# The opening of a two-layer kernel on one core: dummies read a constant, the first block of taps moves ahead of two late transposes, and the early filter turn is split

## The chip, the cores and the metric

The kernel runs on one core of one Trainium2 chip. The core has five engines with instruction streams of their own: PE (matrix multiply; its weight loads are shown as PEld), DVE (vector), ACT (scalar functions, copies), POOL and SP (which only issues transfers here). An engine works through its stream in the order in which the program was written; engines wait for each other through semaphores. The metric is the device time of one execution, in microseconds (us).

## The reference

Two layers, each a gated long convolution followed by a gated feed-forward block, over x of 2048 tokens by 576 channels, all in bf16:

```python
def _A_ref(q, k, v, shift_k, ssm_k, ssm_D):
    k_pad = jnp.pad(k, ((0, 0), (ks - 1, 0), (0, 0)))          # ks = 4 taps
    for t in range(ks):
        k_shift = k_shift + k_pad[:, t:t + S, :] * shift_k[:, ks - 1 - t][None, None, :]
    kv = k_shift * v
    y = irfft(rfft(kv, 2S) * rfft(ssm_k, 2S))[:S]               # along the tokens
    y = y + kv * ssm_D[None, None, :]
    return q * y

def _B_ref(x, w_gate, w_up, w_down):                            # 576 -> 4608 -> 576
    return (_gelu(x @ w_gate) * (x @ w_up)) @ w_down

x = A_q
x = x + _A_ref(_layernorm(x), A_k, A_v, A_shift_k, A_ssm_k, A_ssm_D)
x = x + _B_ref(_layernorm(x), B_w_gate, B_w_up, B_w_down)
x = x + _A_ref(_layernorm(x), A_k, A_v, A_shift_k, A_ssm_k, A_ssm_D)
x = x + _B_ref(_layernorm(x), B_w_gate, B_w_up, B_w_down)
```

The transforms are written out in the kernel as matmuls with tables of cosines and sines. The product with D is folded into the filter: D is added to its value at time 0.

## The kernel before

The 2048 tokens are cut into four blocks of 512. The convolution does block 0 first (`Conv.begin`, L836), as fast as it can, since the feed-forward block of the first 512 tokens needs its result. The other three blocks are then woven into the feed-forward matmuls, in an order that a planner (`Pace`, with estimated costs) writes down when the program is built. The change doesn't touch the planner, and nothing in `begin` that the change edits feeds it. The order within `begin` is written out by hand; each engine follows it.

A block of 512 tokens lies on 128 partitions with RT = 4 tokens each, so token i of a partition is one of 0 to 3. The 576 channels are four full blocks of 128 and one of 64 (nd = 4, `width`). What `begin` does on each engine, as far as the change and the steps below touch it:

- SP issues the loads: k of block 0 (L172), the filter's first 512 channels into `hn` (L875), its last 64 channels, also into `hn` (L876), v (L181), the tables `W`, and later the feed-forward weights.
- **Dummies** (`busy`, L893): matmuls of 128x256 with a result that nobody reads, eight at first and two a little later. They read `full`, a part of `wx[1]` that DVE sets to 1.0 (L867).
- **Tap columns**: matmuls of `sk9` with the identity (L901) give the taps per channel, `wcol`; others (L912) give the taps of the last channels along the partitions, `sx`. DVE makes diagonal matrices `dg` from `wcol` (L907): for channel blocks 0 and 1 all four taps, for block 2 the taps 2 and 3. ACT makes taps 0 and 1 of block 2 later (L970).
- **k turned**: twelve transposes (L930), copied by ACT into `kT` (L935): channel blocks 0 and 1 in one copy, block 2 in another.
- **Late filter turn**, `turn_h(…, 1)`: tokens 3 and 2 of the filter, eight transposes of full channel blocks and then two of the last 64 channels (L963). Then `turn_d` (L937): one small transpose of D (L940), ACT's copy into `dcol` (L942), POOL's addition to the filter at time 0 in `hn` (L944). Then ACT copies the late tokens to `hT0` (L966).
- **Blocks of taps** (`shift_taps`, L819): for each of the channel blocks 0, 1 and 2, seven matmuls of turned k with the diagonals, 2048 columns in all. Blocks 0 and 1 share the one bank pair of the pool `cps`; block 2 has one of the three of the pool `ps`.
- **Early filter turn**, `turn_h(…, 0)`: tokens 1 and 0, ten transposes, written between blocks 0 and 1 and copied by ACT (L966).
- The last 192 channels of the taps go through DVE instead (L948 to L954).
- DVE multiplies the blocks of taps by v (L990), in two instructions: blocks 0 and 1, then block 2.
- **Filter transform**: `even(0, 0)` and `even(0, 1)` (L228) use the tokens 0 and 2 of `hT0`, token 0 first. Then the **transform of kv**, `kfwd` (L219), then `odd` (L228 again), then DVE's differences (`apart`, L233) and products (L359 to L362).

`new()`, `small()`, `new_t()` and `small_t()` take the next bank pair of the pools `ps` (three) and `cps` (one); a bank pair is used again when its last reader is done.

Of the kernel before, what the change touches and what calls it, by code (L numbers as in the profile page):

```python
# [15 lines left out]
ACT = mybir.ActivationFunctionType  # L16
ALU = mybir.AluOpType
F32 = mybir.dt.float32
BF16 = mybir.dt.bfloat16
# [3 lines left out]
P = 128  # L23
# [63 lines left out]
class Conv:  # L87
# [748 lines left out]
    def begin(self, head, tables):  # L836

        tc, nc, D, KS = self.tc, self.nc, self.D, self.KS
        nd = D // P
        width = lambda db: min(P, D - db * P)  # L840
        with ExitStack() as es:
# [8 lines left out]
            nt = nd - 1  # L850
            DW = D - nt * P
            wcol = tmp.tile([P, nt, KS], F32, name="wcol")
            sx = tmp.tile([P, KS, DW], BF16, name="sx")
            warm = tmp.tile([P, 1], F32, name="warm")
# [5 lines left out]
            dg = head.scratch([P, nt, RT, P], "dg")  # L860
            kx = tmp.tile([P, RT + KS - 1, DW], BF16, name="kx")
            below = tmp.tile([P, P], BF16, name="below")
            wx = [tmp.tile([P, RT, DW], BF16, name=f"wx{i}") for i in range(2)]
            full = wx[1][:].rearrange("p i c -> p (i c)")[:, 0:256]

            twice = lambda src: src.unsqueeze(1).to_broadcast([NH, 2, src.shape[1]])
            nc.vector.memset(full, 1.0)  # L867
            nc.scalar.dma_start(out=sk9[:], in_=twice(self.sk.rearrange("(b p) j -> b (p j)", p=HP)))
            self.load_k(0, nc.sync)
            nc.scalar.dma_start(out=dv9[:], in_=twice(self.sD.rearrange("(b p) -> b p", p=HP)))  # L870
            nc.vector.memset(kT[:, :, :, 0:2], 0.0)
            nc.vector.memset(below[:, 0:1], 0.0)
            nc.vector.tensor_copy(out=below[:, 1:P], in_=self.ident[:, 0:P - 1])
            nc.scalar.activation(out=warm[:], in_=full[:, 0:1], func=ACT.Sqrt)
            nc.sync.dma_start(out=hn[:, 0:nd, :], in_=self.hk[0:nd * P, 0:BS].rearrange("(b p) t -> p b t", p=P))  # L875
            nc.sync.dma_start(out=hn[0:D - nd * P, nd, :], in_=self.hk[nd * P:D, 0:BS])  # L876
            self.load_v(0, nc.sync)
# [12 lines left out]
            new_t = lambda: self.psp.tile([P, 2, 1024], BF16, tag="pr", name="pt")  # L890
            small_t = lambda: self.cpsp.tile([P, 2, 1024], BF16, tag="cps", name="cpt")

            def busy(ps, n):  # L893
                for _ in range(n):
                    nc.tensor.matmul(ps[:, 0, 0:256], lhsT=full[:, 0:P], rhs=full, start=True, stop=True)
            idle = small()
            busy(idle, 8)
            ps = new()
            halves = ((0, HP), (HP, P))
            for j in range(KS):  # L900
# [9 lines left out]
            ps = new()  # L910
            for c in range(DW // HP):
                nc.tensor.matmul(ps[:, c // 2, c % 2 * HP * KS:(c % 2 + 1) * HP * KS],  # L912
                                 lhsT=self.ident[0:NH, 2 * nt + c:2 * nt + c + 1].to_broadcast([NH, P]),
                                 rhs=sk9[:, 0, :], start=True, stop=True)
            for e, (lo, hi) in enumerate(((0, P), (P, DW))):
                nc.scalar.copy(out=sx[:, :, lo:hi], in_=ps[:, e, 0:(hi - lo) * KS].rearrange("p (d j) -> p j d", j=KS))
            busy(idle, 2)
            k, v = self.kt_[0], self.vt_[0]
            rest = slice(nt * P, D)
# [4 lines left out]
            pts = []  # L924
            for n, dbs in enumerate(DBS):
                pt = new_t() if n else small_t()
# [6 lines left out]
            for dbs, pt in zip(DBS, pts):  # L933
                ne = len(dbs)
                nc.scalar.copy(out=kT[:, dbs[0]:dbs[-1] + 1, :, 2:P + 2],  # L935
                               in_=pt[:, 0:ne, 0:RT * P].rearrange("p e (u q) -> p e u q", u=RT))
            def turn_d(pt):  # L937

                at = RT * P
                nc.tensor.transpose(pt[:, 1, at:at + NH], dv9[:].rearrange("b h p -> b (h p)"), self.ident[0:NH, 0:NH])  # L940
                for h, (lo, hi) in enumerate(halves):
                    nc.scalar.copy(out=dcol[lo:hi, 0:(NH + 1 - h) // 2], in_=pt[lo:hi, 1, at + h:at + NH:2])  # L942
                for lo, hi, w in ((0, nd, P), (nd, nd + 1, D - nd * P)):
                    nc.gpsimd.tensor_tensor(out=hn[0:w, lo:hi, 0], in0=hn[0:w, lo:hi, 0], in1=dcol[0:w, lo:hi], op=ALU.add)  # L944
# [8 lines left out]
                tt(out=wx[0][:], in0=wx[0][:], in1=wx[1][:], op=ALU.add)  # L953
            tt(out=v[:, :, rest], in0=wx[0][:], in1=v[:, :, rest], op=ALU.mult)  # L954

            def turn_h(pt, g, first=None):

                hv = hn[:].rearrange("p b (q i) -> p b i q", i=RT)
                for dbs in (range(nd), (nd,)):
                    for i in (2 * g + 1, 2 * g):  # L960
                        for db in dbs:
                            w = width(db)
                            nc.tensor.transpose(pt[:, i % 2, db * P:db * P + w], hv[0:w, db, i, :], self.ident[0:w, 0:w])  # L963
                if first:
                    first()
                nc.scalar.copy(out=hT0[:, 2 * g:2 * g + 2, :], in_=pt[:, :, 0:D])  # L966

            turn_h(new_t(), 1, lambda: turn_d(pts[1]))
            for j in range(2):
                nc.scalar.activation(out=dg[:, nt - 1, j, :], in_=self.ident[:], func=ACT.Copy, scale=wcol[:, nt - 1, j:j + 1])  # L970
            out = []
            for n, dbs in enumerate(DBS):
                o = (new() if n else small())[:].rearrange("p e (i c) -> p e i c", i=RT)
                for e, db in enumerate(dbs):
                    self.shift_taps(k, kT, dg, P, db, o[:, e])
                    if db == 0:
                        turn_h(new_t(), 0)
                out.append(o)
            self.hT1 = head.scratch([P, RT, D], "hT1")[:]
            nc.sync.dma_start(out=self.hT1, in_=self.Td[1].rearrange("(p i) d -> p i d", i=RT))  # L980
            skT = tc.dram_tile([1, KS * D], BF16, name="skT")
# [904 lines left out]
```

## Time and profile before

| | |
|---|---|
| runs | 908.52, 909.13, 910.92 us (median 909.13) |
| span of the profiled execution | 908.5 us |
| busy share | PE 99%, PEld 58%, DVE 63%, ACT 36%, POOL 17% |
| the chain that ended last, by engine | PE 97%, DVE 2%, DMA 1% |
| first matmul of gate/up (end of the opening) | 35.22 us |

The span runs from the first to the last instruction of one profiled execution; which of the three times belongs to it is not noted. In the rows below, a timeline row is start, length, engine, line of the kernel, operation, output<-inputs, tile and count; in square brackets stands how long the engine was idle before and what ended this. Rows next to each other on the timeline can be several instructions merged. A row of the chain is start, length, and the engine and line that it ran through. A row of a group by shape is line, engine, operation, shapes, count, then busy us, mean ns of one, and idle us before. PE's matmuls are pipelined: a mean of 0.4 us and a step of 0.2 us from one to the next go together.

### The profile page before, as it was taken

To read this page: it belongs to the slowest core of one execution; us is meant where nothing else is said; L and a number is where in the kernel's file an instruction comes from. 1 tells how busy PE (TensorE), PEld (TensorE's weight loads), DVE (VectorE), ACT (ScalarE), POOL (GpSimd) and SP (SyncE) were. 2 spreads that over 40 slices of the span, in tenths; PEclk is the share of its full clock that TensorE was granted. 3 is DMA by queue.
4 is the path that set the end of the run, shared out by engine and by line. 5 is a ranking of instruction groups with operands and counts; after the bars stand their busy time and mean duration, and the time that the engine had idled before them with its cause. 6 is when DMAs were issued, how large, how long until landed. Compare 5 with 4: busy or idle time off the path is not lost.

```text
span 908.5 us, 19157 instructions
## 1 busy us (share of the span) xinstructions
PE 902.1 (99%) x8133; PEld 524.7 (58%) x8133; DVE 575.9 (63%) x984; ACT 328.8 (36%) x616; POOL 158.2 (17%) x336
## 2 busy tenths in 40 slices
PE   9999999999999999999999999999999999999998
PEld 6875646556465465564654655645646646556555
DVE  7989976688888884787898855443333335332332
ACT  6765455523223254443125133551121125321221
POOL 3333315120223031420104002310000003100000
PEclk9999999999999999999999999999999999999999
DMA  9999997666629319785915601961520721966620
GB/s 260 301 298 295 221 226 139 193 190 147 198 92 266 95 27 172 210 142 131 273 55 133 169 3 42 187 137 41 123 73 15 143 80 27 190 162 172 142 55 27
DMA packets 132075, 132.90 MB, mean 146 GB/s; under 512 B 46139, under 2 KB 123670, under 8 KB 131990
## 3 DMA queue, kind: packets, MB, share of 16 engines
q1 hardware_dynamic: 121728, 94.65, 46.2%
q0 software_dynamic: 10208, 37.02, 13.0%
q8 instruction: 63, 1.03, 0.5%
q14 instruction: 22, 0.18, 0.1%
q10 hardware_dynamic: 54, 0.01, 0.0%
HBM read 108.36 MB, written 12.39 MB: 133 GB/s over the span
## 4 chain that ended last, share of the span: by engine, by line
PE 97%; DVE 2%; DMA 1%; SPq 0%; issue 0%; ACT 0%; DVEq 0%
PE gu L1758 59%; PE dn L1792 31%; PE gu L1677 3%; PE cps L282 1%; PE ps L415 1%; DMA hn<-in_A_ssm_k_dram 1%; PE cps L415 1%; PE ps L282 0%; DVE yb L362 0%; PE cps L823 0%; DVE prod L359 0%; DVE h L233 0%; DVE prod L361 0%; PE xps L1477 0%; DVE v L990 0%; PE pt L963 0%
## 5 line engine op out<-in xcount | busy, mean ns | idle before, releaser
L1758 PE MATMUL gu<-xnT,wgu 64*128 64x512 bf16 x4968 | 540.7, 376 | 0.0
L1758 PEld LDWEIGHTS <-wgu 64*128 64x128 bf16 x4968 | 239.7, 94 | 294.4 <-issue 5.9
L1767 ACT ACTIVATE ga<-gu 128x512 f32<-128x512 f32 x258 | 153.9, 596 | 451.1 <-PE gu L1758 442.7
L1768 DVE TENSOR_TENSOR hT<-ga,gu 128x512 bf16<-128x512 f32 x258 | 177.0, 686 | 200.0 <-ACT ga L1767 198.4
L1792 PE MATMUL dn<-wd,hT 128*128 128x288 bf16 x2304 | 292.1, 286 | 0.0
L1792 PEld LDWEIGHTS <-hT 128*128 128x128 bf16 x2304 | 223.5, 98 | 65.6 <-issue 9.5
L1831 DVE TENSOR_TENSOR x_c<-x_c,dn 128x576 f32<-128x576 f32 x62 | 46.6, 752 | 55.3 <-PE dn L1792 54.9
L1230 POOL TENSOR_SCALAR nm<-s 128x1 f32<-128x1 f32 x56 | 20.4, 365 | 270.5 <-DVE x_c L1823 210.8
L1238 ACT ACTIVATE junk<-x_c,nm 128x576 bf16<-128x576 f32 x48 | 36.9, 768 | 28.0 <-POOL nm L1230 25.9
L560 POOL DMA_DIRECT2D hr<-Hd x32 | 17.4, 545 | 117.7 <-DVE prod L361 117.1
L1246 POOL TENSOR_TENSOR rstd<-ve,neghalf_t 128x1 f32<-128x1 f32 x58 | 36.8, 635 | 4.8
L1302 ACT ACTIVATE xn<-x_c,nb,rstd 128x576 bf16<-128x576 f32 (+1 forms) x48 | 28.6, 644 | 5.9 <-POOL nb L1250 5.7
L1245 POOL TENSOR_SCALAR ve<-ss 128x1 f32<-128x1 f32 x58 | 21.8, 375 | 45.9 <-ACT junk L1238 45.8
L1814 DVE TENSOR_TENSOR ob<-x_c,dn 128x576 bf16<-128x576 f32 x15 | 11.3, 754 | 29.0 <-PE dn L1792 29.0
L285 ACT COPY eo<-cps 128x576 f32<-128x576 f32 x29 | 18.6, 643 | 27.3 <-PE cps L282 24.1
L1656 ACT ACTIVATE ga<-gu 128x512 bf16<-128x512 f32 x26 | 15.5, 598 | 30.5 <-PE gu L1758 25.9
L1677 PE MATMUL gu<-xnT,wgu 64*128 64x256 bf16 x432 | 24.8, 269 | 0.3 <-ACT xnT L1484 0.3
L1677 PEld LDWEIGHTS <-wgu 64*128 64x128 bf16 x432 | 21.4, 94 | 3.2 <-issue 1.2
L362 DVE TENSOR_TENSOR prod<-prod 128x576 bf16<-128x576 bf16 x48 | 22.0, 458 | 1.7
L430 POOL DMA_DIRECT2D out_dram<-ob x12 | 6.7, 562 | 91.6 <-DVE ob L1814 91.6
L245 DVE SCALAR_TENSOR_TENSOR eo<-eo 128x576 f32<-128x576 f32 x22 | 16.3, 753 | 5.8 <-ACT eo L285 5.8
L1280 DVE SCALAR_TENSOR_TENSOR x_c<-g_t,rstd,x_c 128x576 f32<-128x576 f32 x16 | 13.0, 814 | 8.6 <-POOL rstd L1246 8.6
(182 smaller groups left out, 591.3 us busy)
## 6 DMA issues: line engine op xcount, KB each, us to landing
wgu<-in_B_w_gate_dram SPq DMA_DIRECT2D x45, 576.0 KB, 5.6
wd<-in_B_w_down_dram SPq DMA_DIRECT2D x30, 864.0 KB, 7.1
wgu<-in_B_w_up_dram SPq DMA_DIRECT2D x45, 512.0 KB, 7.6
hr<-Hd POOLq DMA_DIRECT2D x32, 288.0 KB, 5.0
kr<-Kd POOLq DMA_DIRECT2D x24, 288.0 KB, 5.3
Kd<-kc POOLq DMA_DIRECT2D x12, 288.0 KB, 6.2
k<-in_A_k_dram POOLq DMA_DIRECT2D x3, 1008.0 KB, 12.0
wgu<-in_B_w_up_dram SPq DMA_DIRECT2D x45, 64.0 KB, 7.7
```

The lines of the kernel that those rows point to most:

```text
L362: nc.vector.tensor_tensor(out=dst, in0=pr[:, 0, :], in1=pr[:, 1, :], op=ALU.subtract if part == 0 else ALU.add)
L1230: nc.gpsimd.tensor_scalar(out=v["nm"][:], in0=v["s"][:], scalar1=-1.0 / D, scalar2=None, op0=ALU.mult)
L1238: nc.scalar.activation(out=junk[:], in_=get_x(), func=ACT.Square, bias=v["nm"][:, 0:1], accum_out=v["ss"][:])
L1245: nc.gpsimd.tensor_scalar(out=ve[:], in0=v["ss"][:], scalar1=1.0 / D, scalar2=EPS, op0=ALU.mult, op1=ALU.add)
L1246: nc.gpsimd.tensor_tensor(out=v["rstd"][:], in0=ve[:], in1=neghalf_t[:, 0:1], op=ALU.pow)
L1302: nc.scalar.activation(out=xn[:, lo:hi], in_=x_c[c][:, j, 0:hi - lo], func=ACT.Identity, scale=v["rstd"][:, 0:1], bias=v["nb"][:, 0:1])
L1677: nc.tensor.matmul(pair[:, s, e * 256:(e + 1) * 256], lhsT=w[r0:r0 + HK, k, gi * P:(gi + 1) * P], rhs=xnT[r0:r0 + HK, blk_of[k], tok], sta ...
L1758: nc.tensor.matmul(pair[:, s, :], lhsT=w[r0:r0 + HK, k, gi * P:(gi + 1) * P], rhs=xnT[r0:r0 + HK, b, :], start=(k == 0), stop=(k == NKC - 1))
L1767: nc.scalar.activation(out=ga[:], in_=pair[:, 0, :], func=ACT.Gelu_apprx_tanh)
L1768: nc.vector.tensor_tensor(out=hT[:, fi, :], in0=ga[:], in1=pair[:, 1, :], op=ALU.mult)
L1792: nc.tensor.matmul(part[h][:, h, 0:HW], lhsT=hT[:, fi, at * P:(at + 1) * P], rhs=wd[2 * wb + fi // WT][:, fi % WT, h * HW:(h + 1) * HW], s ...
L1831: nc.vector.tensor_tensor(out=xh, in0=xh, in1=acc[:, :, 0:HW], op=ALU.add)
```

## The change

The dummies and the table-loading activation read a constant of ones, one element repeated, that the program sets up before it starts; the DVE memset goes, and ten dummies are issued at first, not eight. `turn_h` is cut into the transposes and the copy (`keep_h`). Of the late turn only the eight full transposes stay ahead of the blocks of taps. The two of the last 64 channels, the turn of D, the late copy and ACT's two diagonals of block 2 come after block 0. Of the early turn, token 1 (five transposes) comes after block 1 and token 0 (five) after block 2; one copy follows both.

```diff
-            full = wx[1][:].rearrange("p i c -> p (i c)")[:, 0:256]
+            ones = lambda n: nc.const_aps.tensor(1.0, [P, n], BF16)
...
-            nc.vector.memset(full, 1.0)
...
-            nc.scalar.activation(out=warm[:], in_=full[:, 0:1], func=ACT.Sqrt)
+            nc.scalar.activation(out=warm[:], in_=ones(1), func=ACT.Sqrt)
...
-                    nc.tensor.matmul(ps[:, 0, 0:256], lhsT=full[:, 0:P], rhs=full, start=True, stop=True)
+                    nc.tensor.matmul(ps[:, 0, 0:256], lhsT=ones(P), rhs=ones(256), start=True, stop=True)
             idle = small()
-            busy(idle, 8)
+            busy(idle, 10)
...
-            def turn_h(pt, g, first=None):
+            def turn_h(pt, tokens, dbs):
 
                 hv = hn[:].rearrange("p b (q i) -> p b i q", i=RT)
-                for dbs in (range(nd), (nd,)):
-                    for i in (2 * g + 1, 2 * g):
-                        for db in dbs:
-                            w = width(db)
-                            nc.tensor.transpose(pt[:, i % 2, db * P:db * P + w], hv[0:w, db, i, :], self.ident[0:w, 0:w])
-                if first:
-                    first()
+                for i in tokens:
+                    for db in dbs:
+                        w = width(db)
+                        nc.tensor.transpose(pt[:, i % 2, db * P:db * P + w], hv[0:w, db, i, :], self.ident[0:w, 0:w])
+
+            def keep_h(pt, g):
                 nc.scalar.copy(out=hT0[:, 2 * g:2 * g + 2, :], in_=pt[:, :, 0:D])
 
-            turn_h(new_t(), 1, lambda: turn_d(pts[1]))
-            for j in range(2):
-                nc.scalar.activation(out=dg[:, nt - 1, j, :], in_=self.ident[:], func=ACT.Copy, scale=wcol[:, nt - 1, j:j + 1])
+            late_t = new_t()
+            turn_h(late_t, (3, 2), range(nd))
+            early_t = None
             out = []
             for n, dbs in enumerate(DBS):
                 o = (new() if n else small())[:].rearrange("p e (i c) -> p e i c", i=RT)
                 for e, db in enumerate(dbs):
                     self.shift_taps(k, kT, dg, P, db, o[:, e])
                     if db == 0:
-                        turn_h(new_t(), 0)
+                        turn_h(late_t, (3, 2), (nd,))
+                        turn_d(pts[1])
+                        keep_h(late_t, 1)
+                        for j in range(2):
+                            nc.scalar.activation(out=dg[:, nt - 1, j, :], in_=self.ident[:], func=ACT.Copy, scale=wcol[:, nt - 1, j:j + 1])
+                    elif db == 1:
+                        early_t = new_t()
+                        turn_h(early_t, (1,), range(nd + 1))
                 out.append(o)
+            turn_h(early_t, (0,), range(nd + 1))
+            keep_h(early_t, 0)
```

## The prediction

> **What bounds the kernel now.** First I read the page's busy shares and a table of busy times by stretch, to learn where time can be won at all.
>
> ```profile
> span 908.5 us, 19157 instructions
> PE 902.1 (99%) x8133; PEld 524.7 (58%) x8133; DVE 575.9 (63%) x984; ACT 328.8 (36%) x616; POOL 158.2 (17%) x336
> 40.00:200.00 160.00, 160.00 (x1580) 98.18 (x1578) 130.64 (x228) 81.74 (x159) 51.91 (x101) 1.00 0.89 227
> 200.00:400.00 200.00, 200.00 (x1768) 113.04 (x1765) 163.51 (x277) 78.27 (x147) 46.20 (x94) 1.00 0.65 157
> ```
>
> In the last two rows the columns are the stretch, its length, then busy time of PE, PEld, DVE, ACT and POOL. From 40 us on PE has no gap that the profile shows, and the instructions there are not edited. So what the change does is settled in the opening, and a shift at its end should arrive at the end of the kernel undiminished: the opening would have to lose to nothing that waits for a clock of its own, and behind 40 us only PE's own work sets the pace.
>
> Next the chain that ended last, in its first 36 us (start, length, what).
>
> ```profile
> 1.66 6.04 DMA hn<-in_A_ssm_k_dram
> ...
> 7.74 0.29 PE pt L963 x2
> 8.04 0.12 PE pt L940
> 8.15 1.82 PE cps L823 x7
> 9.97 1.08 PE pt L963 x10
> 11.05 1.33 PE cps L823 x7
> ...
> 12.41 1.83 DVE v L990 x2
> ...
> 14.29 1.14 PE cps L219 x8
> ...
> 16.03 0.75 DVE h L233
> ...
> 28.52 0.47 DVE yb L362
> ...
> 34.48 0.70 ACT xnT L1484
> ...
> 35.22 8.04 PE gu L1677 x144
> ```
>
> The reader is to see three things. The filter's last 64 rows land at 7.70 and PE waits for them. Then PE runs block 0 of the taps, the whole early filter turn (ten transposes) and block 1, and DVE multiplies by v; the first transform of kv (L219) waits for that product. From 16.03 DVE works through a chain without rest until 28.99, and gate/up begins at 35.22. So **the number to forecast is when the transform of kv at 14.29 starts**; everything behind it hangs on the DVE chain, which a stretch of it shows full (DVE is the fourth busy figure after the length, third engine):
>
> ```profile
> 20.00:25.00 5.00, 5.00 (x43) 3.99 (x42) 4.86 (x10) 4.53 (x9) 2.88 (x8) 1.00 1.09 294
> ```
>
> That table writes a granted clock of 1.00 in every stretch, also in the opening, but the matmuls' own durations say otherwise. By shape, for block 0 and 1 (cps) and block 2 (ps):
>
> ```profile
> L823 PE MATMUL cps<-dg,kT 128*128 128x512 bf16 x2 | 1.2, 608 | 0.0
> L823 PE MATMUL ps<-dg,kT 128*128 128x512 bf16 x1 | 0.4, 379 | 0.0
> ```
>
> The same shape takes 608 ns in the first two blocks and 379 ns in the third. PE is slow until about 11.6 us, in the middle of block 1, and I keep that as a second unknown.
>
> **The change part by part.** The rows of the timeline that price it:
>
> ```profile
> 0.80 0.06 DVE L1163 MEMSET eps_t<- 128x1 f32 x1 [0.80 <-PEq L1870]
> 0.91 0.27 DVE L867 MEMSET wx<- 128x256 bf16 x1
> 1.24 1.89 PE L895 MATMUL cps<-wx 128*128 128x256 bf16 x8 [1.24 <-DVE below L872]
> 3.06 0.29 PE L901 MATMUL ps<-ident,sk 9*128 9x6 bf16 x4
> 3.77 1.39 DVE L907 TENSOR_SCALAR dg<-ident,wcol 128x128 bf16<-128x128 bf16 x8
> 5.92 1.01 ACT L935 COPY kT<-cpt 128x1024 bf16<-128x1024 bf16 x1 [0.15 <-PE cpt L930]
> 6.11 1.06 PE L963 MATMUL pt<-ident,hn 128*128 128x128 bf16 x8
> 8.09 1.89 PE L823 MATMUL cps<-dg,kT 128*128 128x512 bf16 x7
> 8.19 0.33 ACT L942 CAST dcol<-pt 64x5 f32<-64x5 bf16 x2 [0.77 <-PE pt L940]
> 8.54 1.12 ACT L966 COPY hT<-pt 128x1152 bf16<-128x1152 bf16 x1
> 9.56 0.69 ACT L970 ACTIVATE dg<-ident,wcol 128x128 bf16<-128x128 bf16 x2
> 9.77 1.29 PE L963 MATMUL pt<-ident,hn 128*128 128x128 bf16 x10
> 10.98 1.39 PE L823 MATMUL cps<-dg,kT 128*128 128x512 bf16 x7
> 11.09 1.12 ACT L966 COPY hT<-pt 128x1152 bf16<-128x1152 bf16 x1 [0.84 <-PE pt L963]
> 12.21 1.03 PE L823 MATMUL ps<-dg,kT 128*128 128x512 bf16 x7
> 13.08 1.14 PE L228 MATMUL ps<-hT,W 128*128 128x288 bf16 x8
> ```
>
> *Dummies.* Eight of them step by (1.89 - 0.42) / 7 = 0.21 us, 0.42 being the mean of one. Without the DVE memset they can start when the first instructions behind the start barrier do, at 0.80 to 0.85. Ten from there have been fed by 0.85 + 2.1 = 2.95; eight from 1.24 were fed by 2.92. The matmuls of the taps (3.06) therefore start at the same time, whether these wait for PE or for their data. The unknown is the operand that repeats one element. The nearest rows are two weight loads of nine rows:
>
> ```profile
> L901 PEld LDWEIGHTS <-sk 9*128 9x128 bf16 x4 | 0.2, 113 | 0.4 <-issue 0.4
> ...
> L912 PEld LDWEIGHTS <-ident 9*128 9x128 bf16 x3 | 0.3, 118 | 0.1
> ```
>
> L912 repeats one column of the identity and takes 118 ns, against 113 ns for the plain load of L901. I take nothing. From above: if streaming it cost double, ten would cost 2.1 us more, and the tap matmuls and the block that needs them would come up to 2.1 us later. Dropping the memset frees 0.27 us of DVE, but DVE's first work on the path, the diagonals at 3.77, hangs on the sk matmuls of 3.06: nothing. The activation that loads the square root table only reads another operand, and nobody waits for its result: nothing.
>
> *Block 0 ahead of the last 64 rows.* It needs the diagonals (3.77 + 1.39 = 5.16), the copy of the turned k (5.92 + 1.01 = 6.93) and PE, which has fed the eight transposes of the late turn by about 6.97. So it starts at 7.05 instead of 8.09, fills PE while the rows land at 7.70, and feeds for 9.77 - 8.09 = 1.68 us, to 8.73. The late turn's two small transposes and the turn of D then take what they took from 7.74 to 8.09, 0.35 us, and block 1 starts at 9.08 instead of 10.98, since the ten early transposes are no longer ahead of it. At the slow rate it ends at 10.76. v's first product on DVE would start about 10.9 instead of 12.41.
>
> *What is queued behind.* ACT now does the column of D, the late copy and two diagonals of block 2 after the turn of D, so later. Before, dcol began 0.10 us after block 0 began and L970 ended 2.16 us after it (10.25 - 8.09); now they count from block 1: ACT is ready with the diagonals at 9.08 + 2.16 = 11.24. Block 2 waits for these. The first part of the early turn (token 1, five transposes) lies there: half of 10.98 - 9.77, 0.60 us, so 10.76 to 11.36. It covers the wait. POOL's addition to hn, which follows dcol, was done by 9.77, at most 1.25 us after dcol's end (8.52); now that is 10.76 at the latest, so it holds up neither early part. Block 2 starts near 11.36, partly slow (until 11.6, some 0.12 us extra), 0.87 us fast by 13.08 - 12.21: it has been fed by 12.35.
>
> *The second part of the early turn.* Token 0's five transposes come now after block 2. What transposes take at the fast rate shows later in the opening:
>
> ```profile
> 33.19 0.67 PE L1477 MATMUL xps<-ident,xn 128*128 128x128 bf16 x9
> ```
>
> Nine take 0.67 us there, against 1.06 us for eight at 6.11; five should take some 0.45, and they end near 12.8. Only then can ACT copy both early tokens (1.12 us, 12.85 to 13.97), and PE's next instruction, the even half of the filter transform (L228), needs token 0 out of that copy. So **PE, which before ran from block 2 straight into L228 at 13.08, now stands from 12.6 to 14.02.** Before, that copy ran at 11.09 to 12.21 beside block 1 and cost nothing; its cover is gone. L228's eight matmuls (two groups) feed for 8 x 0.12 = 0.97 us, and the transform of kv, behind them in PE's order, starts at 15.0 instead of 14.29. v's two products took 1.83 us together; the second can follow block 2 by 12.6 and is over before 13.5, so v no longer matters. The queues of SP and POOL are not passed by any moved step.
>
> Sum: +1.90 won for block 1, all of it lost behind it, and 15.0 - 14.29 = **+0.7 us** for the transform of kv, handed on by the DVE chain to 35.22 and to the end. On the profiled span: 908.5 + 0.7 = 909.2. The runs shown are 908.52, 909.13 and 910.92, so this span stands 0.6 us under their median; on the median the forecast is 909.13 + 0.7 = 909.8. About 0.3%, 2.7 us, is what a measurement of this kernel can tell from no change, so this is no change that can be told.
>
> **The rivals.**
>
> *B, the fast rate comes sooner.* PE went fast some 3.9 us after it took up work without a gap (7.74 to about 11.6), and 7.74 ends the one clear hole:
>
> ```profile
> 7.00:8.00 1.00, 0.42 (x5) 0.18 (x3) 0.93 (x3) 0.42 (x1) 0.00 (x0) 1.00 1.03 396
> ```
>
> Block 0 fills that hole. If the hole kept PE slow, the rate rises about 8.3: a quarter of block 0 runs fast and it is fed by 8.53, block 1 starts 8.85 and ends 9.72, the diagonals are ready at 8.85 + 2.16 = 11.01, block 2 is fed by 11.95, the copy runs 12.4 to 13.5 and the transform of kv starts 14.5: +0.2, or 909.3. ACT, not PE, is then the bound. For it: the hole is gone. Against it: the stretch from 1.24 to 7.17 has no such hole either, and PE stayed slow in it (eight transposes in 1.06 us at 6.11, nine in 0.67 later).
>
> The Trainium skill, "TensorE: Matmul & The Clock Gate", Part 1, says that the array runs at half rate until one free-running window of about 3.4 us was busy; by it alone the rate would already have come by 5 or 8 us, and the trace has it at 11.6. Part 4 of that page says that transposes do not count as busy in that way; the trace fits this (no rise during the 2 us of transposes before 7.17), and by it B falls and the sum stays at +0.7.
>
> *C, slower: the new hole keeps PE slow.* The hole at 12.6 to 14.0, 1.4 us, is longer than that at 7.2. If PE has not gone fast before it, because the short matmuls at 8.73 to 9.08 break the stretch as the sk matmuls of 3.06 may have done, the count starts again at the resumption. Slow against fast is 1.68 - 0.87 = 0.81 us for the 2048 columns of a block. Block 2 then costs 0.7 more and the five transposes 0.2; the hole ends at 14.9; of the twenty matmuls of 288 columns up to the first odd half, sixteen fall into the next 3.9 us, at 0.11 us extra each, 1.8. Together 0.7 + 0.7 + 0.2 + 1.8 = +3.4: 912.5. It decides from the point where the rise has not come by 12.6. Against it: block 0 to block 2 now lie closer together than before.
>
> *D, the fast rate comes from the dummies*, at 0.85 + 3.9 = 4.8. Block 0 is then over before the filter's rows land at 7.70. Block 1 starts at 8.05, the diagonals are ready at 8.05 + 2.16 = 10.2, block 2 is fed by 11.1, the five transposes end at 11.55, the copy at 12.7, and the transform of kv starts at 13.7: -0.6, 908.5. Against it: the dummies of before did not do this with only short gaps behind them.
>
> *E, the repeated operand costs double*: the bound above, +2.1 on the sum, 911.9. The row of L912 speaks against it.
>
> **How the numbers follow.** Forecast (A) 0.47, B 0.25, C 0.15, D 0.08, E 0.05. The likeliest is A, 909.8. Its own range is 908.7 to 911, from the spread of the runs shown. The range of all reaches down to D less the run spread, 908.0, and up to C, 912.6. Slower by over 0.3% (above 911.9) are C and half of E: 0.17. Faster by over 0.3% (under 906.4) is no case of mine; a gain of 2.7 us would be a fifth of the opening to 14.29. For what I have not priced in D and B I leave 0.06. Within 0.3%: 0.77.
>
> **What would show it.** Right: block 0 starts at 7.0 to 7.1, block 1 near 9.1; block 2 directly behind five transposes near 11.4; L228 waits over 1 us for ACT's early copy; the transform of kv starts near 15.0; v's products have long ended. B shows 379 ns for the first matmul of block 1, C shows slow matmuls at L228, E dummies that step by over 0.3 us. Wrong would be: an early copy that ends before 13.1, a DVE chain that starts later than the transform of kv explains, or a gap of PE behind 40 us.

## The result and the profile after

The changed kernel has a median of 910.36 us (909.75 to 910.92, 21 runs), the kernel before 908.78 us (908.17 to 911.24, 21 runs in the same sessions). The ratio is 1.0016, 95% interval 1.0010 to 1.0022: slower by about 1.5 us (0.9 to 2.0 by the interval); the medians are 1.6 us apart. The shortest of the 21 runs differ by as much, 909.75 and 908.17. The time moved as forecast, within 0.3% and upwards, but by twice the 0.7 us of the sum.

The spans of the two profiles seem to say the opposite:

```profile
span 908.1 us, 19161 instructions
...
PE 901.0 (99%) x8135; PEld 524.4 (58%) x8135; DVE 575.8 (63%) x983; ACT 328.9 (36%) x616; POOL 158.8 (17%) x336
```

908.1 is less than the 908.5 of before. Behind the opening nothing has changed: the table by stretch of the changed kernel (stretch, length, busy time of PE, PEld, DVE, ACT, POOL) has PE without a gap as before.

```profile
40.00:200.00 160.00, 160.00 (x1578) 98.06 (x1576) 130.83 (x228) 81.56 (x159) 51.84 (x101) 1.00 0.92 227
```

So the opening decides here too. The chain of the changed kernel that ended last (start, length, what):

```profile
8.72 1.12 ACT hT L964
9.84 0.60 ACT dg L979 x2
10.48 1.03 PE ps L823 x7
...
11.92 1.13 ACT hT L964
13.09 1.14 PE ps L228 x8
...
35.01 5.07 PE gu L1684 x89
```

Before, this stretch of the chain was PE and then DVE's product with v. Now ACT stands in it twice: with the late copy and the diagonals ahead of block 2, and with the early copy alone ahead of the filter transform (L228). Gate/up begins at 35.01 instead of 35.22. That is half of the 0.4 us between the spans; the other 0.2 us comes behind the last piece of the chain, which ends at 905.17 and at 905.38. So in the two profiles the changed kernel's opening is the shorter one, while its median is the longer. The timeline of the changed kernel (start, length, instruction, idle time and its end):

```profile
0.77 2.29 PE L894 MATMUL cps<-const-bfloat16-1.0 128*128 128x256 bf16 x10 [0.77 <-PEq L1877]
...
6.92 1.12 PE L823 MATMUL cps<-dg,kT 128*128 128x512 bf16 x7
...
7.97 0.25 PE L961 MATMUL pt<-ident,hn 64*128 64x64 bf16 x2
...
8.27 1.05 PE L823 MATMUL cps<-dg,kT 128*128 128x512 bf16 x7
...
9.15 0.54 PE L961 MATMUL pt<-ident,hn 128*128 128x128 bf16 x5
9.65 0.56 DVE L953 TENSOR_TENSOR v<-wx,v 128x768 bf16<-128x768 bf16 x1
...
10.23 1.23 DVE L997 TENSOR_TENSOR v<-cps,v 128x1024 bf16<-128x1024 f32 x1
10.48 1.03 PE L823 MATMUL ps<-dg,kT 128*128 128x512 bf16 x7 [0.80 <-ACT dg L979]
...
11.35 0.54 PE L961 MATMUL pt<-ident,hn 128*128 128x128 bf16 x5
...
11.92 1.12 ACT L964 COPY hT<-pt 128x1152 bf16<-128x1152 bf16 x1 [1.49 <-PE pt L961]
...
13.09 1.14 PE L228 MATMUL ps<-hT,W 128*128 128x288 bf16 x8 [1.21 <-ACT hT L964]
...
14.07 1.14 PE L219 MATMUL cps<-v,W 128*128 128x288 bf16 x8
```

The seven matmuls of block 0 took 1.89 us in the first profile of before and take 1.12 us here; block 1 takes 1.05. In this run PE went fast about 7.1 us in, in the first one of before about 11.6. The two profiles differ in this as well as in the change, and PE waits 0.80 us for the diagonals and 1.21 us for the early copy.

### The profile page after: what moved, and what is told of

It reads as the page before. It is cut to its first block, busy times and chain, and to the rows that moved or that the text cites. A ratio compares the mean times of both kernels' runs of the same rounds, so it can differ in the third digit from the quotient of the medians.

```text
span 908.1 us, 19161 instructions
## 1 busy us (share of the span) xinstructions
PE 901.0 (99%) x8135; PEld 524.4 (58%) x8135; DVE 575.8 (63%) x983; ACT 328.9 (36%) x616; POOL 158.8 (17%) x336
## 4 chain that ended last, share of the span: by engine, by line
PE 98%; DVE 1%; ACT 0%; issue 0%; DVEq 0%
PE gu L1765 59%; PE dn L1799 31%; PE gu L1684 3%; PE cps L282 1%; PE ps L415 1%; PE cps L415 1%; PE ps L282 0%; DVE yb L362 0%; PE cps L894 0%; DVE prod L359 0%; DVE h L233 0%; DVE prod L361 0%; ACT hT L964 0%; PE xps L1484 0%; PE ps L228 0%; PE pt L961 0%
```

## The experiments

**Theory (copies):** the change loses because ACT's work, moved behind block 0, is late: block 2 waits for the diagonals, and the early copy stands alone between block 2 and the filter transform. **Rival (rate):** the two kernels only differ in the moment at which PE goes fast, for which the dummies or the hole at 7.2 are to blame. Each experiment has 10 or 11 runs, in three groups of four. The kernel before has a median of 908.72 us beside the first four shown; of 908.53 beside the old dummies put back, block 0 ahead alone, the diagonals made earlier and before without dummies; and of 908.58 beside the rest.

**The kernel before, again.** No edit.

> The kernel before, once more, for a second profile of it. Time minus span is 1.7 us in every run of the changed kernel, so the first profile of before (span 908.5) belongs to a run of about 910.2, above the median of 908.78. Copy theory (the changed kernel loses where ACT's early copy stands alone between block 2 and the filter transform): most runs of before go fast on PE well ahead of 11.6 us; if this profile catches one, the matmuls of block 0 and 1 take 379 ns for 512 columns, the filter transform starts near 11.4, the transform of kv near 12.4 and the span is near 906.6. Rival (the two kernels only differ in when PE goes fast): a profile with fast PE in block 0 and 1 still has the transform of kv near 14, and a span near 908.

908.39 us. Its timeline, with the view's first line:

```profile
core 0 of [0], span 906.4 us
...
7.35 0.25 PE L963 MATMUL pt<-ident,hn 64*128 64x64 bf16 x2 [0.34 <-DMA hn<-in_A_ssm_k_dram]
...
7.65 1.04 PE L823 MATMUL cps<-dg,kT 128*128 128x512 bf16 x7
...
9.25 1.05 PE L823 MATMUL cps<-dg,kT 128*128 128x512 bf16 x7
...
9.71 1.11 ACT L966 COPY hT<-pt 128x1152 bf16<-128x1152 bf16 x1
10.14 1.03 PE L823 MATMUL ps<-dg,kT 128*128 128x512 bf16 x7
10.34 1.23 DVE L990 TENSOR_TENSOR v<-cps,v 128x1024 bf16<-128x1024 f32 x1
...
11.01 1.14 PE L228 MATMUL ps<-hT,W 128*128 128x288 bf16 x8
...
12.21 1.14 PE L219 MATMUL cps<-v,W 128*128 128x288 bf16 x8
```

The same program, 2.1 us shorter than in its first profile, and the transform of kv (L219) starts at 12.21, not at 14.29. Two things differ. The filter's last 64 rows let PE go on at 7.35, not at 7.74, so block 0 starts 0.44 us sooner (7.65 for 8.09); and PE is fast in block 0 (1.04 us against 1.89), which leaves 4.56 us from block 0 to the transform of kv for the 6.20 of the first profile, 1.6 us less. This profile belongs to a run of 908.19 us, so 1.8 us lie around the span. If they do in every run, the first profile, with 908.5, is of a run of about 910.2, longer than all but 7 of the 119 runs of the kernel before that stand beside the changed kernel and the experiments. The copies' theory had this; the rate alone does not explain 14.07 in the changed kernel with a fast block 0.

**The early copy in two.**

```diff
                         turn_h(early_t, (1,), range(nd + 1))
+                        nc.scalar.copy(out=hT0[:, 1:2, :], in_=early_t[:, 1:2, 0:D])
...
-            keep_h(early_t, 0)
+            nc.scalar.copy(out=hT0[:, 0:1, :], in_=early_t[:, 0:1, 0:D])
```

> The changed kernel with the early copy in two: token 1 copied behind its own five transposes, token 0 alone behind block 2. Copy theory: the copy that stands between block 2 and the filter transform shrinks from 1.12 us to about 0.6 us, the filter transform starts 0.5 us sooner (12.6 instead of 13.1 with the rows of the changed kernel) and the time falls by 0.5 us, to 909.9. Rival (when PE goes fast): nothing changes, 910.4.

910.21 us. The timeline of this run:

```profile
12.11 0.54 PE L961 MATMUL pt<-ident,hn 128*128 128x128 bf16 x5
...
12.68 0.64 ACT L986 COPY hT<-pt 128x576 bf16<-128x576 bf16 x1 [0.96 <-PE pt L961]
...
13.37 1.14 PE L228 MATMUL ps<-hT,W 128*128 128x288 bf16 x8 [0.73 <-ACT hT L986]
```

The wait falls from 1.21 to 0.73 us, the 0.5 us that the copies' theory expects for this place. The time that it expected, 909.9, was missed: the median fell by 0.15 us only. The ratio to before, 1.0016 (1.0007 to 1.0025), holds both a gain of 0.5 us and none, so by time this run decides nothing. Its profile has a later fast rate (block 0 takes 1.66 us), and its transform of kv starts no sooner, at 14.35.

**The early turn undivided, behind block 1, its copy beside block 2.**

```diff
-                        turn_h(early_t, (1,), range(nd + 1))
+                        turn_h(early_t, (1, 0), range(nd + 1))
+                        keep_h(early_t, 0)
...
-            turn_h(early_t, (0,), range(nd + 1))
-            keep_h(early_t, 0)
```

> The changed kernel with the early turn undivided: all ten transposes behind block 1, the copy behind them on ACT, block 2 after that. Copy theory: the copy runs at 10.5 to 11.6 beside block 2, the filter transform follows block 2 with hardly a gap (about 11.6), the transform of kv starts near 12.6, and the time falls by 1.4 us to 908.9, as before the change. Rival (when PE goes fast): the time stays at 910.4.

909.14 us, ratio to before 1.0002 (0.9993 to 1.0011). The timeline of this run:

```profile
11.53 1.12 ACT L964 COPY hT<-pt 128x1152 bf16<-128x1152 bf16 x1
11.57 1.03 PE L823 MATMUL ps<-dg,kT 128*128 128x512 bf16 x7
...
12.70 0.83 PEld L228 LDWEIGHTS <-W 128*128 128x128 bf16 x7 [0.33 <-issue]
```

The same whole copy (1.12 us) now runs beside block 2, and the filter transform starts as soon as it ends, with 0.33 us of waiting left on PE's weight loads. (PE went fast late in this run, block 0 took 1.89 us, so its span of 907.7 is not a usual one.) Undoing the split alone gives back 1.2 of the 1.6 us between the medians, and the longest of its 11 runs, 909.64, is below the shortest of the changed kernel's 21, 909.75. This edit bears most of the argument.

**The new dummies alone**, in the kernel before (the edits of the change ahead of `turn_h`).

> The kernel before with the new dummies alone (constant of ones, ten at first, from 0.77 us). Copy theory: the dummies cost nothing and win little; PE still meets the hole at 7.2, so the median stays within 0.3 us of before (908.5 to 909.1). Rival (the dummies change when PE goes fast, and that is the loss): slower by over 1 us, 910. If the dummies bring the fast rate sooner, the runs of 910.5 and more become rarer than the third that before has.

908.72 us, as before. **The old dummies in the changed kernel** (the same lines undone):

> The changed kernel with the dummies of before (eight at first, from the memset). Copy theory: the reordering is the whole loss and the dummies none of it: 910.4, as the changed kernel. Rival (the dummies shift when PE goes fast, and this is part of the loss): 909.5 or less.

910.67 us, ratio to before 1.0024 (1.0014 to 1.0033): the loss is all there. No part of the loss can be seen to come from the dummies, and the rival falls in this form.

**Block 0 ahead, the early turn where it was.**

```diff
                             nc.scalar.activation(out=dg[:, nt - 1, j, :], in_=self.ident[:], func=ACT.Copy, scale=wcol[:, nt - 1, j:j + 1])
-                    elif db == 1:
                         early_t = new_t()
-                        turn_h(early_t, (1,), range(nd + 1))
+                        turn_h(early_t, (1, 0), range(nd + 1))
+                        keep_h(early_t, 0)
...
-            turn_h(early_t, (0,), range(nd + 1))
-            keep_h(early_t, 0)
```

> The changed kernel with the early turn where it was before, whole and between block 0 and block 1; of the reordering only block 0 ahead of the late transposes is left. Copy theory: ACT's diagonals still come late (two copies' time behind the turn of D), so block 2 waits for them and the early copy runs beside block 2; the transform of kv starts at 12.6 with an early fast rate and 13.4 with a late one: median 908.9 to 909.1, so this half of the reordering wins nothing against before (908.7) and loses nothing much; the split costs the other 1.3 us. Rival (block 0 ahead is what costs): 910 or more.

908.94 us, ratio 1.0004 (0.9995 to 1.0013). So block 0 ahead, with ACT's work behind it but without the split, wins nothing. Its chain shows a wait that I had not thought of:

```profile
9.68 0.17 ACT dcol L941
...
9.92 0.34 POOL hn L943
...
10.30 0.57 PE pt L961 x5
```

Directly behind the turn of D, the early transposes wait for D to be copied by ACT and added by POOL (PE's weight loads stand 0.24 us for POOL). In this run, too, PE was slow in block 0 (1.89 us).

**The early turn undivided, and the diagonals made earlier on ACT.** As the undivided early turn, and ACT's two diagonals written ahead of the late turn:

```diff
+            for j in range(2):
+                nc.scalar.activation(out=dg[:, nt - 1, j, :], in_=self.ident[:], func=ACT.Copy, scale=wcol[:, nt - 1, j:j + 1])
             late_t = new_t()
```

> The changed kernel with the early turn undivided behind block 1 (as in the run before) and ACT's two diagonals of block 2 made ahead of the late turn, where ACT stood idle for 1.0 us. So far every profile has its span at 894.1 us plus the start of the transform of kv. Copy theory: block 2 no longer waits for the diagonals, the early copy starts when the early turn ends, and DVE's chain to v becomes the bound; the transform of kv starts at 12.1 to 12.9, by when PE goes fast, the median is 908.4, and no run lies above 909.5. Rival (ACT's queue doesn't matter, only when PE goes fast): as with the undivided early turn alone, 909.1.

908.67 us, ratio 1.0 (0.9991 to 1.0009); no run above 909.23. The timeline of this run:

```profile
7.36 0.70 ACT L967 ACTIVATE dg<-ident,wcol 128x128 bf16<-128x128 bf16 x2
...
10.66 1.05 PE L823 MATMUL ps<-dg,kT 128*128 128x512 bf16 x7
10.77 1.12 ACT L964 COPY hT<-pt 128x1152 bf16<-128x1152 bf16 x1 [0.38 <-PE pt L961]
...
11.94 1.14 PE L228 MATMUL ps<-hT,W 128*128 128x288 bf16 x8 [0.23 <-ACT hT L964]
```

Block 2 waits for nothing, L228 for 0.23 us. With the wait for the diagonals gone and that for the copy down to 0.23 us the loss is gone, but the kernel before is not beaten.

DVE's list shows why little is to be won. In the first profile of the changed kernel its product for the last 192 channels (L953) ends at 10.21, and v's first product (L997) starts at 10.23, though block 1 was done at 9.3. The 1.83 us of v's two products put the transform of kv at about 12.1 at the earliest (an estimate from these rows), and the second profile of before already has it at 12.21.

**Block 0, D and the diagonals first.** The turn of D and the diagonals ahead of block 0, the early turn whole behind the late one; and the same without any dummies.

```diff
             turn_h(late_t, (3, 2), range(nd))
+            turn_d(pts[1])
+            for j in range(2):
+                nc.scalar.activation(out=dg[:, nt - 1, j, :], in_=self.ident[:], func=ACT.Copy, scale=wcol[:, nt - 1, j:j + 1])
...
                         turn_h(late_t, (3, 2), (nd,))
-                        turn_d(pts[1])
                         keep_h(late_t, 1)
...
+                        early_t = new_t()
+                        turn_h(early_t, (1, 0), range(nd + 1))
+                        keep_h(early_t, 0)
```

> Block 0 ahead of the last 64 rows, as in the change, but the turn of D and ACT's two diagonals ahead of block 0, and the early turn whole behind the late one, ahead of block 1. Copy theory: both copies of the filter run beside blocks 0 and 1, nothing waits for ACT, block 2 follows block 1 at once, and the transform of kv waits for v alone: its start is 12.1 to 12.6 whenever PE goes fast, the median 908.0 to 908.3, below before (908.5 to 908.8) by what the hole at 7.2 is worth, 0.3 to 0.5 us. Rival (block 0 ahead gains nothing even without ACT's waits): 908.6 or more.

> The run before without any dummies. The tap columns come 0.75 us sooner, as they did when the dummies of the kernel before were left out, so DVE's chain does too. If PE then goes fast as soon as with dummies: the transform of kv starts near 12 and the median is 907.8 to 908.2. If the dummies bring the fast rate sooner: 908.5 or more.

908.61 us (ratio 1.0002, 0.9994 to 1.0011) and 908.92 us (1.0009, 1.0000 to 1.0017). Both expectations of a gain fail. (908.5 or more was expected of the second if the dummies bring the fast rate; the number fits, but in its profile block 0 is fast without them, 1.04 us.) One run of the first lies at 910.59 and three of eleven of the second above 910.6, while the longest of the 33 of the kernel before beside them is 909.92. Without dummies the tap columns came 0.46 us sooner (2.87 for 3.33), not 0.75, since the taps themselves land at 2.54 there, and the transform of kv started at 12.60. The timeline of the first:

```profile
7.43 0.16 PE L939 MATMUL pt<-ident,dv 9*128 9x9 bf16 x1 [0.31 <-ACT kT L934]
...
7.52 1.89 PE L823 MATMUL cps<-dg,kT 128*128 128x512 bf16 x7
...
11.01 1.89 PE L823 MATMUL cps<-dg,kT 128*128 128x512 bf16 x7
...
12.69 1.32 PE L823 MATMUL ps<-dg,kT 128*128 128x512 bf16 x7
...
14.83 1.14 PE L219 MATMUL cps<-v,W 128*128 128x288 bf16 x8
```

The turn of D writes the bank pair that holds the turned k of block 2, waits for ACT's copy of it, and block 0 behind it starts at 7.52 instead of 6.92. This profile also shows a late fast rate: blocks 0 and 1 take 1.89 us each, PE is fast only inside block 2. That run took 910.59 us against the median of 908.61.

**The moment of the fast rate.** Two runs in the order of before: all dummies left out (the matmuls whose result nobody reads), and six unread transposes of the identity put into the hole at 7.2.

> The kernel before without any dummies (the eight and the two left out; their result is not read). If the dummies bring the fast rate nearer, it comes later than in the profiles of before, 10 us or more, and the median rises by 0.5 to 1.5 us to 909.2 to 910.2. If they do nothing, it stays at 908.7.

> The kernel before with six unread transposes of the identity in the hole at 7.2 where PE waits for the last 64 rows. If the hole is what makes PE go fast late in some runs, no run lies above 909.5 and the median falls by 0.2 us or more (908.5 or less). If it isn't, the median stays (908.5 to 908.8) and runs of 910 and more can still be seen.

908.59 us (ratio 0.9999, 0.9990 to 1.0008) and 908.71 us (1.0002, 0.9993 to 1.0011): neither moved the median. Of the kernel before, none of the 65 runs beside these two was as long as 910 us, so they cannot say whether dummies or hole make the late rate rarer. The changed kernel once more:

> The changed kernel once more. The profile catches PE going fast at some other moment; the transform of kv starts between 13.9 and 15.0, the filter transform waits over 1 us for the early copy in any case, and the span is 894.0 us plus the start of the transform of kv. Median 910.4.

910.64 us, ratio 1.0021 (1.0012 to 1.0030); L228 waits 1.21 us again, the transform of kv starts at 14.41, the span is 908.4. The run with the filled hole is of use in another way. It went fast in those six transposes, at the moment at which the first profile of the changed kernel did, and has the order of before:

```profile
core 0 of [0], span 906.6 us
...
7.04 0.53 PE L962 MATMUL pt<-ident 128*128 128x128 bf16 x6
...
7.80 1.04 PE L823 MATMUL cps<-dg,kT 128*128 128x512 bf16 x7
...
8.68 0.79 PE L966 MATMUL pt<-ident,hn 128*128 128x128 bf16 x10
...
9.40 1.05 PE L823 MATMUL cps<-dg,kT 128*128 128x512 bf16 x7
...
10.29 1.03 PE L823 MATMUL ps<-dg,kT 128*128 128x512 bf16 x7
...
11.16 1.14 PE L228 MATMUL ps<-hT,W 128*128 128x288 bf16 x8
...
12.36 1.14 PE L219 MATMUL cps<-v,W 128*128 128x288 bf16 x8
```

At like rate the transform of kv starts at 12.36 in the order of before and at 14.07 in the changed one, 1.7 us apart, and the spans are 906.6 and 908.1, 1.5 us apart (the 0.2 us at the end again), close to the 1.6 us between the medians. Step by step, from L228 to L228 (11.16 and 13.09, +1.93): block 0 starts 0.88 sooner (6.92 for 7.80; 0.14 of it lies ahead of the reordering, since the filter's turn starts at 6.04 for 6.18); it feeds 0.17 longer, since PE is slow in its first part (6.92 to 7.97, for 7.80 to 8.68); the late transposes and the turn of D now lie behind it, 0.30 (7.97 to 8.27); the ten early transposes take 0.35 longer, 0.53 and 0.54 (9.15 to 9.68, 11.35 to 11.89) for 0.72 (8.68 to 9.40), since each five are counted to the end of the last one, ahead of a wait; and PE waits 0.80 for the diagonals and 1.21 for the early copy. -0.88 + 0.17 + 0.30 + 0.35 + 0.80 + 1.21 = +1.95, which is the 1.93 but for rounding. From L228 to the transform of kv the changed kernel is 0.22 shorter (0.98 for 1.20), since in the order of before that transform still waits for v's second product; hence 1.7.

## Why the prediction was right in direction and half the size

**The chain and what it hands on: right.** In all profiles of the study the span is the start of the transform of kv plus 894.0 to 894.3 us (14.29 and 908.5; 12.21 and 906.4; 14.07 and 908.1; 14.83 and 908.8): 894.2 to 894.3 with the memset of the old dummies, 894.0 without it. The cause of these 0.2 us at the end is open. A microsecond in the opening is a microsecond at the end. (In the row of 20 to 25 us DVE's 4.86 is the third busy figure behind the length, not the fourth.)

**Block 0 ahead: right.** It started at 6.92 for the 7.05 forecast, and block 1 at 8.27 for 9.08, sooner as PE was fast. DVE did not start on v when block 1 was done, as forecast, but when its own list let it, at 10.23.

**The early copy without cover: right.** PE was forecast to stand for 1.4 us (12.6 to 14.02) ahead of L228; that counts from the end of feeding, and from the forecast end of the transposes, 12.8, it is 1.2. Both profiles of the changed kernel show 1.21 us there, for that copy. Undoing the split gave 1.2 us back.

**The diagonals: covered in the forecast, not on the chip.** Token 1's five transposes were to fill PE from 10.76 to 11.36, just until the diagonals. That would hold for slow PE. With fast PE block 1 ends sooner, and ACT's two copies do not: the wait is 0.80 us. Rival B had this bound (ACT, not PE, sets block 2). Its 2.16 us from the start of block 1 to the diagonals is what the profile shows (8.27 to 10.43); it had block 1 0.6 us too late, and so the transform of kv 0.4 us too late (14.5 for 14.07).

**The baseline: wrong, and this is the step that failed.** The prediction put "this span stands 0.6 us under their median" and added 0.7 us to it. A span is not a time: about 1.75 us lie around it (909.82 and 908.1; 908.19 and 906.4). So the span of 908.5 belongs to a run of about 910.2, and the 14.29 from which the sum was made is 1 to 2 us later than in the other profiles of that order (12.21; 12.81 with the new dummies; 13.24 without any, in the longest of eleven runs). So the term 15.0 - 14.29 was mis-sized: the changed kernel's 14.07 and 14.41 have to be compared with some 12.2 to 13.2. By the medians, less the 1.75 us around the span and the 894 us behind, the transform starts at about 12.8 before and 14.6 after (an estimate): the 15.0 was 0.4 too late, the 14.29 1.5. ACT's copies take 1.12 us at either rate of PE (the one at 8.54 in the first profile of before, the one at 8.72 in the changed kernel), so more of them stands uncovered where PE is fast. A sum made for the rarer slow opening found half of the loss. No profile caught the changed kernel with a slow opening, so its 15.0 for that case was not tested.

**Luck.** That the forecast of 909.8 lies within 0.6 us of 910.36 is in part luck: the median of the three runs, 909.13, was 0.35 us above the 908.78 of 21 runs, and this made up for some of the 0.9 us that the sum lacked.

**The rivals.** B came true as to the rate, but the rate came early for both kernels, and for the kernel before, going by the times, in most runs; its cause, the filled hole, is not shown: the second profile of before went fast at 6.7 us, ahead of the hole. Nor did the 3.9 us from taking up work to the fast rate, with which the prediction counted, hold: with block 0, D and the diagonals first PE took up work at 7.43 and went fast at 13.2. For the 8.3 us of B the prediction shows no working.

In the run with the filled hole the k and filter transposes ran from 4.9 us on, the eight of the filter at a mean of 310 ns and the six unread ones behind them at 225 ns, so the rate rose with nothing but transposes in the 2 us ahead, as its groups by shape show:

```profile
L966 PE MATMUL pt<-ident,hn 128*128 128x128 bf16 x8 | 1.1, 310 | 0.0
...
L962 PE MATMUL pt<-ident 128*128 128x128 bf16 x6 | 0.5, 225 | 0.0
```

Block 0, D and the diagonals first without dummies shows it over a longer stretch. PE waits 0.82 us for k and does two other matmuls (L918); then come only transposes, of k from 4.74, of the filter from 6.02 and of D at 7.39; and block 0 takes 0.98 us in the chain, for 1.82 in the first profile of before:

```profile
4.31 0.64 PE ps L918 x2
...
7.55 0.98 PE cps L823 x7
```

By Part 4 of "TensorE: Matmul & The Clock Gate" in the Trainium skill, transposes do not count as busy; the prediction used this against B. These two runs speak against that rule.

C (the new hole keeps PE slow) did not happen in either profile of the changed kernel. E (the repeated operand costs double) is out: ten dummies in 2.29 us step by 0.21 us, as the old ones did. The opposite sign, a gain, was priced by D at -0.6 us from a fast rate at 4.8; no profile has it before 6.6.

**Open:** what sets the moment of the fast rate. It was seen between about 6.7 us (the second profile of before, inside the filter's transposes) and 13.2 us (inside block 2), in programs that differ little, and at 6.7 and 11.6 us in two executions of the very same one. Neither the dummies nor the hole at 7.2 moved the medians by more than 0.2 us, and block 0, D and the diagonals first went fast ahead of 7.5 with no dummies at all.

## What to carry to other kernels

A copy that runs beside another engine's work costs nothing until the work that covers it is moved; when a step is split and its last part goes behind the cover, the whole copy shows. Before a sum is made on a profile, its run should be placed among the runs by time, not by span, and where two executions of one program differ in a rate, the sum should be made for both. Moving one engine's work forward gains only as much as the slowest queue beside it allows: here ACT's list of copies and diagonals, and DVE's list up to v.

## What the runs showed of the hardware

The matrix engine of one and the same program took 1.89 us for block 0 in one execution and 1.04 us in another, because its rate rose at 11.6 us in the one and 6.7 us in the other. From block 0 to the transform of kv this is worth 1.6 us (6.20 and 4.56), as much as the change; the other 0.4 us between the two spans (908.5 and 906.4) is the filter's last rows, for which PE waits until 7.74 and 7.35. The column of the granted clock wrote 1.00 throughout. The Trainium skill, "TensorE: Matmul & The Clock Gate", Part 1, says that the moment varies from run to run because the activity window runs free of the kernel's start; the runs agree that it varies, but with 4.9 us between two executions of one program by far more than the 0.5 us to either side that the page gives; the reason that the page gives is not tested here.
